# Six ScalarE copies and one in-place transpose instead of six VectorE transposes, for each pair of heads

## The chip, the cores and the metric

The kernel runs on one core of a Trainium2 chip. The metric is the device time of one execution in microseconds (us). A core has five engines with a queue each, worked off in order: TensorE (PE in the profile, with PEld for its weight loads), VectorE (DVE), ScalarE (ACT), GpSimd (POOL) and SyncE (SP, which here issues nearly all DMAs). An instruction that waits holds up everything behind it on its own engine.

## The reference

Eight batches of 576 tokens go through windowed attention with eight heads of 64, and the result through a feed-forward layer. Cut to what matters:

```
masks = [rel >= 0 and rel < 32]  for heads 0-3,  [0 <= rel < 128 and rel % 4 == 0]  for heads 4-7
attn  = softmax(where(mask, q @ k.T / 8, -1e9))        # 576 x 576 for each batch and head
x     = (attn @ v), heads side by side                 # 4608 tokens x 512
g     = elu(x @ w_in)                                  # w_in 512 x 2048
out   = g @ w_out                                      # w_out 2048 x 512
```

Every query sees 32 keys, so a group of 32 queries needs 64 neighbouring keys only (for the dilated heads after a reordering of the tokens).

## The kernel before

**Feed-forward.** The 4608 tokens make nine chunks of 512. Operands are split into a rounded high part and a rest (`wh`, `wl`, `xh`, `xl`, `gh`, `gl`), so that three fast products stand for one exact one. Chunks 0 to 2 do this tile by tile over the 16 blocks of the hidden layer (`product1`, `elu`, `second_product`): PE makes a hidden block in a PSUM bank (`h0`), ACT copies it to SBUF (`L716`, tile `h`), exp and relu (`L721`, `L730`) and a VectorE step (`L731`) make the elu, ACT casts it to `gh` (`L735`), VectorE takes the rest `gl` (`L736`), and two blocks later PE multiplies them with `w_out` into four banks `o_ps`, one for each 128 tokens. At the end of a chunk ACT copies the four banks out (`store`, `L755`, `e<-o_ps`), and the next chunk's products start in the same four banks. Chunks 3 to 6 (`combined_chunk`) use a seven-product scheme (Strassen's) in four groups a chunk: products go to the banks `h0` and `h1`, ACT copies `h0` between products (`e<-h`), and queued second products fill the time between them. Chunks 7 and 8 are done together by `wide_chunks`.

**Attention.** Batch 0 is done at the start, batch 1 inside chunk 0, batches 2 and 3 inside chunks 1 and 2, batches 4 to 7 from the end of chunk 2 to chunk 6. Heads go in pairs, four pairs a batch. For a pair, PE makes scores; VectorE adds the mask into `sm`, 96 partitions (3 groups of 32 queries) x 12 (2 heads x 6 units) x 64 keys; max, subtract, exp (ACT), sum, reciprocal and a multiply make the probabilities (`L415` in `normalise`, or the last 0.9 step of `later_probabilities`). PE then needs them with keys on the partitions: tile `pt`, 128 keys x 12 units x 96 queries, two of them (`pt0`, `pt1`, taken in turn by `transposed`). Group `c` of 32 queries fills column block `c` at partition blocks `c` and `c+1`; all else in `pt` stays at the zeros that were written once at the start. Before the change, VectorE makes each of these six pieces by a transpose from `sm` to `pt` (32 partitions x 12 x 32). In batch 1 this is `L544`, in batches 2 and 3 `L558` (`softmax`, a generator whose steps the main loop draws block by block through `spread`), in batches 4 to 7 it comes from `later_probabilities` (`L573` is the line of a helper, `Ordered`, through which all engine calls of chunks 3 to 8 pass).

**What sets the order.** All matmuls, and everything issued through `Ordered` or `inorder`, stand in program order. The rest (`softmax`, `elu` of chunks 1 and 2, `store`) is placed on its engine by the framework's scheduler, from its own estimate, held only by `issue_after` hints. In chunks 3 to 6 the attention steps wait in a list `side`; at the `w` marks of `TODO` the function `work` takes steps until their listed costs use up the budget in `SPARE`. Steps of pairs 2 and 3 from the transposes on lie in `held` until the outputs of pairs 0 and 1 are issued. `sm` is a single buffer for chunk-1 and chunk-2 pairs.

Of the kernel before, what the change touches and what calls it, by code (L numbers as in the profile page):

```python
# [25 lines left out]
G = 32  # L26
# [60 lines left out]
def body(ctx: ExitStack, tc: tile.TileContext, q, k, v, masks, w_in, w_out, out, out_t):  # L87
    nc = tc.nc
# [101 lines left out]
    def slots(name, *at):  # L190

        step = at[1] - at[0] if len(at) > 1 else 1
        return room_of(name)[:, at[0]:at[-1] + 1:step, :]
# [153 lines left out]
    last_transpose = [None] * B  # L347
# [64 lines left out]
    def normalise(eng, sm, sums, keep):  # L412
        keep(nc.vector.tensor_scalar(out=sums, in0=sums, scalar1=1e-9, scalar2=None, op0=ALU.add))
        keep(nc.vector.reciprocal(out=sums, in_=sums))
        return keep(eng.tensor_tensor(out=sm, in0=sm, in1=sums.unsqueeze(2).broadcast_to([QB, 2 * NU, 2 * G]), op=ALU.mult))  # L415

    def transposed():
        count[0] += 1
        return pt[count[0] % len(pt)]
# [78 lines left out]
    def masks_added(hp, places, sm, eng=nc.vector):  # L498

        dil = hp >= NPAIR // 2  # L500
        for i in range(max(len(p) for p in places)):
            for h in range(2):
                n0, n1, s_ps = places[h][i]
                last = eng.tensor_tensor(out=sm[:, h * NU + n0:h * NU + n1, :].rearrange("p n j -> p (n j)"), in0=s_ps[:QB, :(n1 - n0) * 2 * G],
                                        in1=mask_sb[:, int(dil), n0 * 2 * G:n1 * 2 * G], op=ALU.add)
        return last

    def exponentials(b, hp, places, sm=None):

        if sm is None:  # L510
            sm = ap.tile([QB, 2 * NU, 2 * G], F32, name="sm", bufs=1)
            last = masks_added(hp, places, sm)
            if b == 1:
                masked.append(last.ins)
        nmx = ap.tile([QB, 2 * NU], F32, name="nmx", bufs=4)
        sums = ap.tile([QB, 2 * NU], F32, name="sums", bufs=4)
        with tc.issue_after(rests[0] if (b, hp) == (1, 0) else masked[-1]):
            nc.vector.tensor_reduce(out=nmx, in_=sm, op=ALU.max, axis=mybir.AxisListType.X)
        if b == 1:

            maxima.append(nc.vector.tensor_scalar(out=nmx, in0=nmx, scalar1=-0.125, scalar2=None, op0=ALU.mult).ins)
            if hp > 0:
                for u in range(NU):
                    exponential(u, sm, nmx, sums)
        else:
            nc.vector.tensor_tensor(out=sm, in0=sm, in1=nmx.unsqueeze(2).broadcast_to([QB, 2 * NU, 2 * G]), op=ALU.subtract)
            nc.scalar.activation(out=sm, in_=sm, func=AF.Exp, scale=0.125)
            nc.vector.tensor_reduce(out=sums, in_=sm, op=ALU.add, axis=mybir.AxisListType.X)
        return b, hp, sm, nmx, sums

    def probabilities(b, hp, sm, nmx, sums):
# [12 lines left out]
                    last_transpose[b] = nc.vector.transpose(out=tr[ks, :, cs], in_=sm[cs, :, rs]).ins  # L544
        return b, hp, tr

    spread = []

    def softmax(b, hp, places, tr):

        _, _, sm, _, sums = exponentials(b, hp, places)
        normalise(nc.vector, sm, sums, lambda ins: ins)
        yield
        for c in range(GU):
            for r in range(2):
                ks, cs, rs = slice((c + r) * G, (c + r + 1) * G), slice(c * G, (c + 1) * G), slice(r * G, (r + 1) * G)
                with tc.issue_after(low[-1]):
                    last_transpose[b] = nc.vector.transpose(out=tr[ks, :, cs], in_=sm[cs, :, rs]).ins  # L558
                if (c, r) == (1, 0):
                    yield  # L560
        yield

    def three():
# [11 lines left out]
    vec, act = Ordered(nc.vector), Ordered(nc.scalar)  # L575
    side, held = [], []
# [8 lines left out]
    def later_probabilities(b, hps, groups):  # L585

        other_sm = slots("a5", 2, 3).rearrange("p o t -> p (o t)")[:QB, :2 * NU * 2 * G].rearrange("p (u j) -> p u j", u=2 * NU)
        sms = [ap.tile([QB, 2 * NU, 2 * G], F32, name="sm", bufs=1), other_sm]
        for j in (1, 0):
            masks_added(hps[j], groups[j], sms[j], vec)  # L590
        small = [[ap.tile([QB, 2 * NU], F32, name=n, bufs=4) for n in ("nmx", "sums")] for _ in hps]
        trs = [transposed() for _ in hps]
        wide = lambda x: x.unsqueeze(2).broadcast_to([QB, 2 * NU, 2 * G])

        def steps(j):

            sm, (mx, sums), tr = sms[j], small[j], trs[j]
            yield 0.9, lambda: vec.tensor_reduce(out=mx, in_=sm, op=ALU.max, axis=mybir.AxisListType.X)
            yield 0.9, lambda: vec.tensor_tensor(out=sm, in0=sm, in1=wide(mx), op=ALU.subtract)
            yield 0.0, lambda: act.activation(out=sm, in_=sm, func=AF.Exp, scale=0.125)  # L600
            yield 0.9, lambda: vec.tensor_reduce(out=sums, in_=sm, op=ALU.add, axis=mybir.AxisListType.X)
            yield 0.1, lambda: vec.tensor_scalar(out=sums, in0=sums, scalar1=1e-9, scalar2=None, op0=ALU.add)
            yield 0.1, lambda: vec.reciprocal(out=sums, in_=sums)
            yield 0.9, lambda: vec.tensor_tensor(out=sm, in0=sm, in1=wide(sums), op=ALU.mult)
            for c in range(GU):
                for r in range(2):
                    ks, cs, rs = slice((c + r) * G, (c + r + 1) * G), slice(c * G, (c + 1) * G), slice(r * G, (r + 1) * G)
                    yield 0.57, lambda ks=ks, cs=cs, rs=rs: vec.transpose(out=tr[ks, :, cs], in_=sm[cs, :, rs])

        one, other = list(steps(0)), list(steps(1))  # L610
        side.extend([*one[:2], other[0], one[2], other[1], one[3], other[2], *one[4:7], *other[3:7]])
        (held if hps[0] else side).extend(one[7:] + other[7:])
        return [(b, hp, tr) for hp, tr in zip(hps, trs)]

    def scores_piece(b, hps, between=None):
# [23 lines left out]
        if b <= CS:  # L639
            trs = [transposed() for _ in hps]  # L640
            made = [(b, hp, tr) for hp, tr in zip(hps, trs)]
            one, other = [softmax(b, hp, groups[j], trs[j]) for j, hp in enumerate(hps)]
            next(one)
            spread.extend(((one,), (one, other), (other,), (other,)))
        else:
            made = later_probabilities(b, hps, groups)
# [23 lines left out]
    hidden, below, low, high = [], [], [], []  # L670
# [824 lines left out]
```

## Time and profile before

| | |
|---|---|
| median of three runs | 854.6 us (854.01 to 854.99) |
| the profiled execution | 853.85 us |
| its span, first to last instruction | 852.0 us |
| PE busy, matmuls | 839.9 us (99%) |
| PE weight loads | 704.0 us (83%) |
| VectorE busy | 657.6 us (77%), 993 instructions |
| ScalarE busy | 486.5 us (57%), 835 instructions |
| chain of waits, share of PE | 97% |

The times in the tables of the trace are those of the one profiled execution. A row gives a start, a length, the engine, the line, what is written from what, the size and a count; in brackets stands how long the engine had been idle before it and what ended that. A matmul row's length includes its passage through the array, so that consecutive matmuls overlap: what counts for PE is the distance from start to start.

### The profile page before, as it was taken

What the parts mean: (1) busy time and instruction counts of PE and PEld (TensorE: products, weight loads), DVE (VectorE), ACT (ScalarE), POOL (GpSimd) and SP (SyncE); (2) the same over time, 40 slices, a digit from 0 to 9 for tenths busy, and PEclk for the clock granted to TensorE, in tenths of its full rate; (3) what the DMA queues carried; (4) which work ended last, traced back from release to release, by engine and by line L of the source; (5) the groups of instructions that cost most, each with busy time, mean ns of one, the idle gap of its engine ahead of it and who ended that gap; (6) DMA issues with size and microseconds to landing.
All of it is one profiled execution on the core that took longest, in us unless ns stands there. A gap on an engine that the chain in (4) does not pass through costs nothing.

```text
span 852.0 us, 17515 instructions
## 1 busy us (share of the span) xinstructions
PE 839.9 (99%) x7080; PEld 704.0 (83%) x7080; DVE 657.6 (77%) x993; ACT 486.5 (57%) x835; POOL 8.7 (1%) x29
## 2 busy tenths in 40 slices
PE   6999999999999999999999999999999999999998
PEld 4566888888888889898999899899989988888886
DVE  5999998778588978965877587757877765786992
ACT  5889776645655465434644464544544556786460
POOL 3000000000000000000000000000000000000000
PEclk9999999999999999999999999999999999999999
DMA  8997457533677878757586667767675667997675
GB/s 301 378 378 304 138 170 237 163 112 107 204 253 237 266 206 258 242 181 244 179 262 195 193 219 221 251 186 218 193 237 189 212 209 240 334 353 247 188 222 170
DMA packets 99728, 193.73 MB, mean 227 GB/s; under 512 B 8800, under 2 KB 52160, under 8 KB 99648
## 3 DMA queue, kind: packets, MB, share of 16 engines
q1 hardware_dynamic: 99504, 192.30, 69.5%
q8 instruction: 56, 0.92, 0.4%
q10 hardware_dynamic: 144, 0.31, 0.1%
q14 instruction: 24, 0.20, 0.1%
HBM read 145.39 MB, written 47.19 MB: 226 GB/s over the span
## 4 chain that ended last, share of the span: by engine, by line
PE 97%; DMA 1%; ACT 1%; DVE 1%; issue 0%; SPq 0%; DVEq 0%; POOL 0%; ACTq 0%
PE o_ps L124 44%; PE h L124 41%; PE a_ps L124 11%; DMA r<-w_in 1%; DMA qt<-q 0%; ACT pt L490 0%; DVE nmx L450 0%; PE a L124 0%; DVE pt L488 0%; PE b L124 0%; PE d L124 0%; DVE sums L469 0%; ACT r L467 0%; DVE gh L573 0%; ACT x L404 0%
## 5 line engine op out<-in xcount | busy, mean ns | idle before, releaser
L124 PE MATMUL h<-xh,r 128*128 128x256 f32 (+1 forms) x728 | 171.7, 315 | 0.0
L124 PEld LDWEIGHTS h<-xh,r 128*128 128x128 f32 x728 | 123.6, 190 | 10.5 <-issue 0.2
L124 PE MATMUL o_ps<-a,r 128*128 128x512 f32 x528 | 127.0, 391 | 0.0
L124 PEld LDWEIGHTS o_ps<-a,r 128*128 128x128 f32 x528 | 97.3, 188 | 19.2
L124 PE MATMUL h<-xl,r 128*128 128x256 f32 (+1 forms) x364 | 109.0, 315 | 0.0
L124 PE MATMUL h<-a,r 128*128 128x256 f32 (+1 forms) x492 | 77.7, 308 | 0.0
L124 PE MATMUL o_ps<-a,gh 128*128 128x512 f32 x216 | 75.0, 444 | 0.0
L124 PEld LDWEIGHTS h<-a,r 128*128 128x128 f32 x492 | 69.6, 190 | 6.6
L124 PEld LDWEIGHTS h<-xl,r 128*128 128x128 f32 x364 | 69.3, 190 | 5.7 <-issue 0.2
L573 DVE SCALAR_TENSOR_TENSOR a-1_3460<-a-1_3460,a 128x1024 f32<-128x1024 f32 x32 | 39.1, 1222 | 37.3 <-ACT a L573 37.2
L573 ACT COPY e<-h 128x512 f32<-128x512 f32 x48 | 28.2, 588 | 56.3 <-PE h L124 55.5
L124 PE MATMUL o_ps<-r,r 128*128 128x512 f32 x220 | 57.5, 390 | 0.0
L124 PEld LDWEIGHTS o_ps<-a,gh 128*128 128x128 f32 x216 | 40.2, 188 | 17.3 <-issue 10.5
L573 DVE TENSOR_TENSOR a-1_3460<-h,e 128x512 f32<-128x512 f32 x48 | 33.0, 688 | 26.1 <-PE h L124 25.4
L124 PEld LDWEIGHTS o_ps<-r,r 128*128 128x128 f32 x220 | 40.6, 188 | 8.0
L573 ACT COPY a-1_3460<-h 128x512 f32<-128x512 f32 x16 | 9.4, 586 | 56.2 <-PE h L124 56.2
L124 PE MATMUL h<-r,r 128*128 128x256 f32 (+1 forms) x252 | 40.6, 311 | 0.0
L573 ACT ACTIVATE a<-a 128x1024 f32<-128x1024 f32 (+1 forms) x40 | 40.0, 1017 | 0.9
L716 ACT COPY h<-h 128x512 f32<-128x512 f32 x30 | 17.5, 584 | 39.8 <-PE h L124 39.6
L124 PE MATMUL o_ps<-r,gh 128*128 128x512 f32 x128 | 40.1, 395 | 0.0
L736 DVE TENSOR_TENSOR gl<-e,gh 128x512 fp32r<-128x512 f32 x37 | 25.4, 687 | 17.6 <-ACT gh L735 17.2
L124 PE MATMUL o_ps<-a,a 128*128 128x512 f32 x156 | 38.9, 391 | 0.0
(266 smaller groups left out, 1711.1 us busy)
## 6 DMA issues: line engine op xcount, KB each, us to landing
r<-combined SPq DMA_DIRECT2D x140, 512.0 KB, 4.4
vt<-v SPq DMA_DIRECT2D x30, 384.0 KB, 4.5
kt<-k SPq DMA_DIRECT2D x29, 304.0 KB, 4.3
qt<-q SPq DMA_DIRECT2D x30, 288.0 KB, 3.7
r<-w_in SPq DMA_DIRECT2D x16, 512.0 KB, 7.0
r<-w_out SPq DMA_DIRECT2D x16, 512.0 KB, 8.0
r<-sums_out SPq DMA_DIRECT2D x16, 512.0 KB, 4.7
r<-plain_out SPq DMA_DIRECT2D x12, 512.0 KB, 4.7
```

What stands on the lines that cost most here:

```text
L124: return inorder(nc.tensor.matmul(*args, **kw))
L573: return lambda *args, **kw: inorder(getattr(self.eng, name)(*args, **kw))
L716: copied.append(a.copy(out=h, in_=h_ps).ins)
L736: low.append(v.tensor_tensor(out=gl, in0=e, in1=gh.bitcast(F32), op=ALU.subtract).ins)
```

## The change

For batches 2 to 7 (24 pairs of heads) each of the six VectorE transposes becomes a ScalarE copy of the same 32 x 12 x 32 piece to the same place in `pt`, not yet transposed (`placed`). One VectorE transpose over the whole of `pt` (128 partitions x 1152), with the same tile as input and output, then turns every 32 x 32 block in place (`turned`). Blocks of zeros stay zeros. Batch 1 keeps its six transposes.

```diff
+    def placed(tr, sm, c, r, eng):
+
+        return eng.copy(out=tr[(c + r) * G:(c + r + 1) * G, :, c * G:(c + 1) * G], in_=sm[c * G:(c + 1) * G, :, r * G:(r + 1) * G])
+
+    def turned(tr, eng):
+
+        flat = tr.rearrange("p u q -> p (u q)")
+        return eng.transpose(out=flat, in_=flat)
+
     def softmax(b, hp, places, tr):
...
         yield
         for c in range(GU):
             for r in range(2):
-                ks, cs, rs = slice((c + r) * G, (c + r + 1) * G), slice(c * G, (c + 1) * G), slice(r * G, (r + 1) * G)
-                with tc.issue_after(low[-1]):
-                    last_transpose[b] = nc.vector.transpose(out=tr[ks, :, cs], in_=sm[cs, :, rs]).ins
-                if (c, r) == (1, 0):
-                    yield
+                with tc.issue_after(high[-1]):
+                    placed(tr, sm, c, r, nc.scalar)
+        yield
+        with tc.issue_after(low[-1]):
+            last_transpose[b] = turned(tr, nc.vector).ins
         yield
...
             for c in range(GU):
                 for r in range(2):
-                    ks, cs, rs = slice((c + r) * G, (c + r + 1) * G), slice(c * G, (c + 1) * G), slice(r * G, (r + 1) * G)
-                    yield 0.57, lambda ks=ks, cs=cs, rs=rs: vec.transpose(out=tr[ks, :, cs], in_=sm[cs, :, rs])
+                    yield 0.3, lambda c=c, r=r: placed(tr, sm, c, r, act)
+            yield 1.4, lambda: turned(tr, vec)
...
-        (held if hps[0] else side).extend(one[7:] + other[7:])
+        (held if hps[0] else side).extend(one[7:-1] + other[7:-1] + one[-1:] + other[-1:])
```

The new functions shift the lines below them by nine: `L716` to `L755` of before are `L725` to `L764` now, and `L573` is `L582`. The order of PE's instructions is the same in both programs. On ScalarE and VectorE it is not. At the start of chunk 1, ScalarE had this order before (`a_` and `r_` are weight tiles; the four `e<-o_ps` copies empty the output banks of chunk 0):

```order
L721 ACTIVATE e<-h 128x512
L755 COPY e<-o_ps 128x512 x3
L730 ACTIVATE e<-e 128x512
L716 COPY h<-h_1690 128x512
L755 COPY e<-o_ps 128x512
L721 ACTIVATE e<-h 128x512
L735 CAST gh<-e 128x512
```

and has this one now:

```order
L730 ACTIVATE e<-h 128x512
L764 COPY e<-o_ps 128x512 x3
L739 ACTIVATE e<-e 128x512
L549 COPY pt_80<-sm 32x12x32 x6
L725 COPY h<-h_1693 128x512
L764 COPY e<-o_ps 128x512
L744 CAST gh<-e 128x512
```

The six copies of the first pair of batch 2 stand ahead of the copy of the hidden block and of the fourth output bank's copy. At the first group of chunk 3, ScalarE had before (`a_2290` is the exp tile of the elu, and later the second pair's probabilities; `h_3843` is bank `h0`):

```order
L573 ACTIVATE a_2290<-a_2290 128x1024
L755 COPY e<-o_ps 128x512
L573 COPY e<-h_3843 128x512
L573 CAST r_1178<-a-1_3460 128x1024
L755 COPY e<-o_ps 128x512
L573 ACTIVATE a_2290<-a-1_3460 128x1024
L755 COPY e<-o_ps 128x512 x2
L573 ACTIVATE a_2290<-a_2290 128x1024
L573 COPY e<-h_3843 128x512
```

and has now:

```order
L582 COPY pt_80<-sm 32x12x32 x4
L764 COPY e<-o_ps 128x512
L582 CAST r_1178<-a-1_3468 128x1024
L582 COPY pt_80<-sm 32x12x32
L582 COPY e<-h_3853 128x512
L582 ACTIVATE a_2294<-a-1_3468 128x1024
L764 COPY e<-o_ps 128x512 x2
L582 ACTIVATE a_2294<-a_2294 128x1024
L582 COPY pt_80<-sm 32x12x32
L582 COPY pt_79<-a_2294 32x12x32 x3
L764 COPY e<-o_ps 128x512
L582 COPY e<-h_3853 128x512
```

Five copies into `pt` and a cast stand ahead of the bank's copy `e<-h`, and nine in all ahead of the fourth `e<-o_ps`. The other pairs of batches 2 and 3 show six copies in a row, each time behind an exp or relu (`L730`, `L739`) of a hidden block and ahead of ScalarE's next copy or cast.

## The prediction

> **What bounds the kernel now.** I read the page first, its busy times and the chain of waits:
>
> ```profile
> PE 839.9 (99%) x7080; PEld 704.0 (83%) x7080; DVE 657.6 (77%) x993; ACT 486.5 (57%) x835; POOL 8.7 (1%) x29
> PE 97%; DMA 1%; ACT 1%; DVE 1%; issue 0%; SPq 0%; DVEq 0%; POOL 0%; ACTq 0%
> ```
>
> PE is the path: 97% of the chain that ended last is PE working. Where it idles is told by the view by windows (length, then PE, PEld, DVE, ACT, POOL busy, the granted clock and the DMAs):
>
> ```profile
> 0.00:30.00 30.00, 21.64 (x494) 16.45 (x494) 20.88 (x40) 18.33 (x59) 7.58 (x17) 0.94 0.91 311
> 126.00:325.00 199.00, 198.96 (x1724) 163.49 (x1723) 156.97 (x280) 114.60 (x210) 0.48 (x5) 1.00 0.64 201
> 325.00:690.00 365.00, 365.00 (x3472) 328.02 (x3471) 271.19 (x412) 183.33 (x259) 0.67 (x7) 1.00 0.69 216
> ```
>
> Of 12.1 us that PE is not busy, 8.4 lie in the first 30 us, ahead of the change. From 126 to 690 us, where all 24 changed pairs are worked, PE lacks 0.04 us of 564. VectorE is busy 79% and 74% there, and what it saves cannot shorten a queue that never waits for it. So the question is only whether ScalarE, busy 58% and 50%, can take the copies without making PE wait.
>
> **What the change costs each engine.** The groups by line and shape give the prices (count, busy us, mean ns):
>
> ```profile
> L573 DVE STREAM_TRANSPOSE pt<-a 32x384 f32<-32x384 f32 x48 | 27.3, 568 | 0.8
> L558 DVE STREAM_TRANSPOSE pt<-sm 32x384 f32<-32x384 f32 x48 | 27.3, 568 | 0.7
> L573 DVE STREAM_TRANSPOSE pt<-sm 32x384 f32<-32x384 f32 x48 | 27.2, 568 | 0.8
> L573 DVE SCALAR_TENSOR_TENSOR a-1_3460<-a-1_3460,a 128x1024 f32<-128x1024 f32 x32 | 39.1, 1222 | 37.3 <-ACT a L573 37.2
> L686 ACT CAST xh<-x 128x384 fp32r<-128x384 f32 x4 | 2.0, 508 | 0.0
> L490 ACT COPY pt<-c 32x192 f32<-32x192 f32 x8 | 2.5, 311 | 0.2
> L755 ACT COPY e<-o_ps 128x512 f32<-128x512 f32 x12 | 6.5, 588 | 4.5 <-DMA out<-e 3.8 <-PE o_ps L124 0.7
> ```
>
> VectorE loses 144 transposes of 568 ns, 81.8 us. One of 1152 elements a partition replaces six of 384. At no more than 1222 / 1024 = 1.19 ns an element, from the nearest long VectorE row, 768 more elements make 568 + 914 = 1.48 us, 36 us for 24 pairs; VectorE gains 46 us. The bound below is a single 568 (if the length did not count), the bound above six times 568, 3.4 us, if the width in partitions counted.
>
> ScalarE gains 144 copies of 384 elements a partition from SBUF to SBUF. The nearest row is the cast of 128x384, 508 ns. Below it lies the 192-element copy with 311 ns, above it the 512-element one with 588. What a copy occupies also depends on how it overlaps with its neighbour:
>
> ```profile
> 15.67 2.65 ACT L490 COPY pt<-c 64x192 f32<-64x192 f32 x8
> 140.08 1.54 ACT L755 COPY e<-o_ps 128x512 f32<-128x512 f32 x3
> ```
>
> Three full-width copies of 588 take 1.54, a step of 0.48: each starts 0.1 before its forerunner ends. Eight copies into `pt`, which move from one partition block to another, take 2.65, a step of 0.33 for a length of 0.31: no overlap. The new copies move on by a block, on one side or the other, each time, so I take 0.51 + 0.02 = 0.53 as their step, 3.2 us for six. 144 x 0.508 are 73 us of busy time more for ScalarE, which would stand at 66%.
>
> The Trainium skill (ScalarE: Activation LUTs, What ACT_TABLE_LOAD costs) gives an ACTIVATE 186 ns + 0.833 ns an element and lets neighbours overlap by about 93 ns. By it a copy of 384 would take 506 ns, as the 508 row says, but step by 0.41; the `pt<-c` row contradicts the overlap for this kind of copy.
>
> **Where 3.2 us in one piece reach PE.** The scheduler puts the copies behind ScalarE's work for one hidden block and ahead of the next copies that free a PSUM bank. All later rows of the queue wait. I go through the tight places; elsewhere the copy behind them isn't wanted for longer.
>
> *A, start of chunk 1: the fourth output bank.*
>
> ```profile
> 140.82 0.95 DVE L415 TENSOR_TENSOR sm<-sm,sums 96x768 f32<-96x768 f32 x1
> 141.50 0.64 ACT L730 ACTIVATE e<-e 128x512 f32<-128x512 f32 x1
> 142.71 0.59 ACT L716 COPY h<-h 128x512 f32<-128x512 f32 x1 [0.56 <-PE h L124]
> 143.19 0.59 ACT L755 COPY e<-o_ps 128x512 f32<-128x512 f32 x1
> 144.32 0.41 PEld L124 LDWEIGHTS o_ps<-r,gh 128*128 128x128 f32 x2
> 144.55 0.62 PE L124 MATMUL o_ps<-r,gh 128*128 128x512 f32 x2
> ```
>
> Today the bank is empty at 143.78, and PE loads weights for it at 144.32 (0.23 ahead of its matmul): cover 0.54, and 0.56 of idle before `h`. Now six copies start at 142.04 and end at 142.04 + 5 x 0.53 + 0.51 = 145.20; `h` runs 145.22 to 145.81, the bank's copy 145.71 to 146.30. PE is late by **2.0**.
>
> *B, 247 us: bank `h0`, which chunks 1 and 2 have once.*
>
> ```profile
> 241.76 0.64 ACT L730 ACTIVATE e<-e 128x512 f32<-128x512 f32 x1
> 243.31 0.95 DVE L415 TENSOR_TENSOR sm<-sm,sums 96x768 f32<-96x768 f32 x1
> 247.13 0.39 PE L124 MATMUL h<-xh,a 128*128 128x512 f32 x1
> ```
>
> ScalarE is free at 242.40, but the copies wait for the probabilities, ready at 244.26. Six run to 247.45, then `h` to 248.06; PE wants the bank at 246.90. That is 1.2 late at most; VectorE, with less to do, may have the probabilities sooner. I take **1.0**, from 0.4 up.
>
> *C, 298 us: the cast `gh`.*
>
> ```profile
> 290.62 0.85 ACT L527 ACTIVATE sm<-sm 96x768 f32<-96x768 f32 x1 [2.20 <-DVE sm L526]
> 294.58 0.63 ACT L730 ACTIVATE e<-e 128x512 f32<-128x512 f32 x1
> 294.68 0.95 DVE L415 TENSOR_TENSOR sm<-sm,sums 96x768 f32<-96x768 f32 x1
> 295.12 0.60 ACT L735 CAST gh<-e 128x512 fp32r<-128x512 f32 x1
> 297.99 0.61 PE L124 MATMUL o_ps<-a,gh 128*128 128x512 f32 x2
> 298.65 0.50 PE L124 MATMUL o_ps<-a,gl 128*128 128x512 f32 x1
> ```
>
> With the probabilities at 295.63 the copies end at 298.82 and the cast, now behind them, at 299.46, for a weight load at 297.76: 1.7 late. But here VectorE is the late one (the exp waited 2.20 us for it), and it has lost 2 us of work a pair, so the copies start earlier. Between 0 and 1.7 I take **0.8**.
>
> *D and E, first group of chunk 3.*
>
> ```profile
> 333.54 1.06 ACT L573 ACTIVATE a<-a 128x1024 f32<-128x1024 f32 x1
> 335.35 0.59 ACT L755 COPY e<-o_ps 128x512 f32<-128x512 f32 x1 [0.74 <-PE o_ps L124]
> 336.78 0.59 ACT L573 COPY e<-h 128x512 f32<-128x512 f32 x1 [0.85 <-PE h L124]
> 337.26 1.05 ACT L573 CAST r<-a-1_3460 128x1024 fp32r<-128x1024 f32 x1
> 339.65 1.08 ACT L755 COPY e<-o_ps 128x512 f32<-128x512 f32 x2
> 338.65 1.59 PE L124 MATMUL h<-a,r 128*128 128x256 f32 x12
> 340.08 2.91 PE L124 MATMUL o_ps<-a,r 128*128 128x512 f32 x12
> ```
>
> The relu ends at 334.60. In the new order follow four copies (to 336.60), an output bank (337.21), the cast (337.11 to 338.16), the fifth copy (338.69) and `e<-h` (339.30), which PE wants at 338.42: **0.9** (D). Then exp (to 340.39), two output banks (341.37), relu (342.36), four copies (344.48), and the fourth output bank, at 345.09. PE comes to its fourth block of three matmuls at 340.08 + 9 x 0.227 - 0.23 = 341.9, with D at 342.8: **2.3** (E).
>
> In the later chunks the order puts four copies ahead of the third `e<-h` of a group, and eight behind it. The chain, merged, gives the room:
>
> ```profile
> 396.62 2.75 PE o_ps L124 x12
> 399.37 2.87 PE h L124 x24
> ```
>
> 24 matmuls are two products, 1.44 each. The bank is wanted again two products and 12 second products later, 2.87 + 2.75 = 5.6 us, for 4 x 0.53 + 0.6 = 2.7 us of ScalarE. That cover holds; if it went, each of the seven such places would cost what the copies exceed it by.
>
> VectorE's other new wait: the next pair's mask add (`L504`) needs `sm`, which the copies now hold until they end, and the in-place transpose waits for the sixth copy. Behind both stand only `L731`, `L736` and the softmax itself, and the outputs come six blocks later; I cost it at nothing, at up to 1 us if the transpose took 3.4.
>
> SP issues in order too: the stores `out<-e` of A and E wait for the late bank copies, and the loads behind them by up to 3 us.
>
> ```profile
> r<-combined SPq DMA_DIRECT2D x140, 512.0 KB, 4.4
> ```
>
> Those loads are issued four products ahead and land in 4.4 us; four products with their second products last over 8 us by the two chain rows, so this too costs nothing unless the delay passes 3.6 us.
>
> Sum: 2.0 + 1.0 + 0.8 + 0.9 + 2.3 = 7.0 us. PE has no slack behind these places, so nothing is caught up. The profiled execution would go from 853.85 to 860.9; the median of before lies 0.75 above its profiled execution, so I predict **861.6** (chance 0.66, from 859 to 865). With 0.61 a copy (the 588 row) A to E make about 9.3, with 0.33 (the 311 row) about 2.0: 863.9 and 856.6.
>
> **The rivals.** *The copies overlap* (0.16): step 0.41, and the copy behind starts 0.12 earlier too. A shrinks to 1.2, B and C to 0.3 together, D and E to 2.0: 3.5 us, **858.1**. For it: full-width copies overlap. Against it: the `pt<-c` row, though its source is PSUM. The Trainium skill's overlap, given above, points the same way.
>
> *The cover holds* (0.10), not slower: ScalarE takes the copies into its idle time, and VectorE's 46 us end the little lateness that the trace puts on it, as with `gl` at 298.65 (0.50 instead of 0.39). Price: below 0.5 us in all, **854.1**. It decides only if six copies fit the 1.1 us of cover at A, 0.18 a copy, which is below every row shown. The Trainium skill (Perfetto Trace Analysis, Identifying the Most-Contended Engine) says that matmul busy time is no measure of headroom and to go by weight loads, 83% here, which would leave PE far more to win. Against it the merged row above: 12 matmuls of 512 columns in 2.75 us, one every 0.23, the same distance as inside every full batch.
>
> *The transpose or ScalarE's load bites more* (0.08): at 3.4 us a transpose, or with copies late in the later groups too, 3 to 5 us more, around **866**.
>
> **How the numbers follow.** About 0.2% (1.7 us) is what a measurement of this kernel can tell from no change. The forecast, the overlap and the third rival are slower by more: 0.90. The cover's 0.10 I split into 0.07 the same and 0.03 faster. The range 857 to 865 leaves out the cover and most of the third rival.
>
> **What would show it.** Right: ScalarE copies `pt<-sm` near 508 ns, stepping by 0.53; PE gaps near 144, 247, 298, 338 and 342 us, ended by ACT (or long matmul rows there), nothing new after 345; VectorE's busy time down by about 46 us. Wrong: a copy step of 0.41 or less, PE whole at A and E, or PE waiting for `pt` itself.

## The result: 9.0 us slower

| | before | with the change |
|---|---|---|
| median of four runs | 854.62 us (854.01 to 854.99) | 863.65 us (862.82 to 864.90) |
| ratio, 95% interval | | 1.0108 (1.009 to 1.0125) |
| profiled execution | 853.85 us | 863.18 us |
| its span | 852.0 us | 861.3 us |
| predicted | | 861.6 us, 857 to 865 |

The kernel became slower, as forecast, and by 2 us more than forecast. The busy times and the chain of waits of the new page:

```profile
PE 840.9 (98%) x7080; PEld 702.4 (82%) x7080; DVE 607.1 (70%) x873; ACT 559.0 (65%) x979; POOL 8.7 (1%) x29
...
PE 80%; DVE 7%; ACT 6%; DMA 4%; issue 2%; DVEq 0%; SPq 0%; ACTq 0%
```

VectorE lost 50.5 us of work and ScalarE gained 72.5. PE has the same 840 us to do, but it is no longer the whole chain. The groups by line and shape of the new kernel show what the new operations cost:

```profile
L549 ACT COPY pt<-sm 32x384 f32<-32x384 f32 x48 | 24.4, 509 | 4.1 <-DVE sm L415 3.6
...
L582 DVE STREAM_TRANSPOSE pt<-pt 128x1152 f32<-128x1152 f32 x16 | 21.9, 1370 | 3.3 <-ACT pt L582 3.3
```

A copy takes 0.51 us, a turn 1.37. Now the five places. These are PE's rows of the new kernel's timeline (start, length, and in brackets how long PE had nothing in its array, and what ended that):

```profile
146.50 0.73 PE L124 MATMUL o_ps<-r,gh 128*128 128x512 f32 x2 [1.88 <-ACT e L764]
...
250.77 0.50 PE L124 MATMUL h<-xh,a 128*128 128x512 f32 x1 [1.34 <-ACT h L725]
...
302.58 0.73 PE L124 MATMUL o_ps<-a,gh 128*128 128x512 f32 x2 [0.61 <-ACT gh L744]
...
344.11 1.69 PE L124 MATMUL h<-a,r 128*128 128x256 f32 x12 [0.65 <-ACT e L582]
...
349.84 1.47 PE L124 MATMUL o_ps<-a,r 128*128 128x512 f32 x3 [1.98 <-ACT e L764]
```

They are A, B, C, D and E of the prediction, each ended by ScalarE with the copy or cast that was named. The bracket counts from the end of the last matmul's passage, which overlaps the next start by 0.16 (a matmul row is 0.39 long where one starts every 0.23), so PE lost 0.16 more than it says: 2.04, 1.50, 0.77, 0.81 and 2.14, together 7.3 us. To this each restart adds about 0.1 (the two matmuls behind a gap take 0.73, where they took 0.62 at 144.55 before; the single one 0.50 instead of 0.39). The prediction's own rows tell the same from another side: the matmul of A started at 144.55 before and starts at 146.50 now, that of B at 247.13 and 250.77, of C at 297.99 and 302.58, of D at 338.65 and 344.11.

So far the span would be 7.8 us longer. It is 9.3, and the rest stands right behind E. The view by windows (window, then its length and PE, PEld, DVE, ACT, POOL busy, the granted clock and the DMAs) of the new kernel:

```profile
346.65:350.05 3.40, 1.42 (x7) 0.88 (x6) 2.52 (x2) 3.30 (x7) 0.00 (x0) 1.00 0.92 234
350.05:353.45 3.40, 3.40 (x77) 2.38 (x77) 0.50 (x1) 2.80 (x5) 0.10 (x1) 0.50 0.36 136
353.50:356.90 3.40, 3.40 (x86) 2.71 (x85) 1.40 (x3) 0.00 (x0) 0.00 (x0) 1.00 0.02 5
```

For 3.4 us after the wait at E the granted clock is 0.50. The same matmuls start 7.70 us later than before at the beginning of this stretch and 9.21 later at its end: **1.5 us**, which no term of the prediction had. From there on to the end of the kernel the distance stays between 9.2 and 9.4. All this is the one profiled execution; the other three show a mean granted clock of 0.993 or 0.994 where this one has 0.998, which is about two more stretches of 3.4 us at half clock, and no trace tells where these lay.

What stands ahead of the late bank copies on ScalarE, at A and at D and E, from the new kernel's timeline:

```profile
142.24 3.11 ACT L549 COPY pt<-sm 32x384 f32<-32x384 f32 x6
145.37 0.59 ACT L725 COPY h<-h 128x512 f32<-128x512 f32 x1
145.86 0.59 ACT L764 COPY e<-o_ps 128x512 f32<-128x512 f32 x1
...
342.94 0.51 ACT L582 COPY pt<-sm 32x384 f32<-32x384 f32 x1
343.47 0.59 ACT L582 COPY e<-h 128x512 f32<-128x512 f32 x1
...
347.09 0.51 ACT L582 COPY pt<-sm 32x384 f32<-32x384 f32 x1
347.62 1.55 ACT L582 COPY pt<-a 32x384 f32<-32x384 f32 x3
349.20 0.59 ACT L764 COPY e<-o_ps 128x512 f32<-128x512 f32 x1
```

Six copies take 3.11 us: (3.11 - 0.51) / 5 is a step of 0.52, with no overlap. At A the bank is empty at 146.45, and PE starts at 146.50; at E it is 349.79 and 349.84.

### The profile page after: what moved, and what is told of

Its sections match the earlier page's. It is cut to its first block, busy times and chain, and to the rows that moved or that the text cites. A ratio compares the mean times of both kernels' runs of the same rounds, so it can differ in the third digit from the quotient of the medians.

```text
span 861.3 us, 17540 instructions
## 1 busy us (share of the span) xinstructions
PE 840.9 (98%) x7080; PEld 702.4 (82%) x7080; DVE 607.1 (70%) x873; ACT 559.0 (65%) x979; POOL 8.7 (1%) x29
## 4 chain that ended last, share of the span: by engine, by line
PE 80%; DVE 7%; ACT 6%; DMA 4%; issue 2%; DVEq 0%; SPq 0%; ACTq 0%
PE o_ps L124 36%; PE h L124 33%; PE a_ps L124 10%; DMA qt<-q 1%; DMA r<-w_out 1%; DVE pt L544 1%; ACT pt L549 1%; DMA r<-w_in 1%; ACT e L764 1%; DVE a L177 1%; DMA out<-e 0%; ACT sm L496 0%; DVE gl L745 0%; DVE r L216 0%; ACT h L725 0%
## 5 line engine op out<-in xcount | busy, mean ns | idle before, releaser
L582 DVE SCALAR_TENSOR_TENSOR a-1_3468<-a-1_3468,a 128x1024 f32<-128x1024 f32 x32 | 39.1, 1223 | 50.5 <-ACT a L582 50.5
L582 DVE TENSOR_TENSOR a-1_3468<-h,e 128x512 f32<-128x512 f32 x48 | 33.1, 689 | 42.6 <-PE h L124 42.0
L582 ACT COPY e<-h 128x512 f32<-128x512 f32 x48 | 28.2, 588 | 46.9 <-PE h L124 41.8
L582 ACT ACTIVATE a<-a 128x1024 f32<-128x1024 f32 (+1 forms) x40 | 40.0, 1017 | 0.9
L124 PEld LDWEIGHTS h<-r,r 128*128 128x128 f32 x252 | 35.7, 190 | 4.0 <-issue 0.3
L124 PE MATMUL a_ps<-a,r 128*128 128x512 f32 x156 | 37.3, 389 | 0.0
```

Of the source, the lines that this page charges most:

```text
L124: return inorder(nc.tensor.matmul(*args, **kw))
L582: return lambda *args, **kw: inorder(getattr(self.eng, name)(*args, **kw))
```

## The experiments

The theory is the prediction's: the time is lost at five places, because of what stands behind the copies in ScalarE's queue. Its main rival is that more work on ScalarE, or more traffic, costs something wherever it stands. In what was expected, the half clock is put at 1.1 us, which was my first reading; the rows above give 1.5.

### One half of the pairs alone

In the first kernel `softmax` (batches 2 and 3) is that of before again, in the second the steps of `later_probabilities` (batches 4 to 7) are:

```diff
# late batches only, in softmax; the second kernel undoes the change to later_probabilities in the same way
-                with tc.issue_after(high[-1]):
-                    placed(tr, sm, c, r, nc.scalar)
-        yield
-        with tc.issue_after(low[-1]):
-            last_transpose[b] = turned(tr, nc.vector).ins
+                ks, cs, rs = slice((c + r) * G, (c + r + 1) * G), slice(c * G, (c + 1) * G), slice(r * G, (r + 1) * G)
+                with tc.issue_after(low[-1]):
+                    last_transpose[b] = nc.vector.transpose(out=tr[ks, :, cs], in_=sm[cs, :, rs]).ins
+                if (c, r) == (1, 0):
+                    yield
```

> Only batches 4 to 7 keep the copies and the turn in place; batches 2 and 3 have their six VectorE transposes again. *Five places* (mine: the time is lost where copies stand in ScalarE's queue ahead of a copy or cast that PE wants): A 2.0, B 1.5 and C 0.8 vanish, D 0.8 and E 2.1 stay, and so does the stretch of half clock behind E, which costs about 1.1: 854.6 + 4.1 = 858.7 us, PE waiting only at D and E in 126 to 690 us. *Rival, spread load* (the cost lies in ScalarE's load and in SBUF traffic, and goes with the number of copies wherever they stand): 16 of 24 pairs keep theirs, two thirds of 9.0, so 860.6 us, with PE's gaps spread thinly.

> Only batches 2 and 3 keep the copies; batches 4 to 7 have their VectorE transposes again. *Five places*: A 2.0, B 1.5, C 0.8 stay, D and E vanish, and with them the half clock behind E: 854.6 + 4.3 = 858.9 us. *Spread load*: 8 of 24 pairs, a third of 9.0: 857.6 us. The two terms of this run and of the one with the late batches alone should add up to the whole, 9.0, by either; a shortfall of about 1 would say that the half clock needs both.

Measured against 854.15 us for before: 858.51 us with the late batches alone, ratio 1.0045 (1.0027 to 1.0063), and 858.63 with the early ones, 1.005 (1.0031 to 1.0069). That is 4.4 and 4.5 us, together 8.8 of the 9.0. The five places ask for 4.1 and 4.3, the spread load for 6.0 and 3.0: with twice as many pairs the late batches do not cost more than the early ones. By the intervals the late batches cost 2.3 to 5.4 us and the early ones 2.6 to 5.9, so that the spread load's 6.0 is ruled out and its 3.0, taken alone, is not. PE and windows of the kernel with the late batches alone:

```profile
345.22 1.61 PE L124 MATMUL o_ps<-a,r 128*128 128x512 f32 x3 [1.96 <-ACT e L764]
```

```profile
17.65:21.00 3.35, 3.35 (x45) 3.32 (x43) 3.25 (x7) 1.98 (x6) 1.16 (x2) 0.50 1.03 357
...
341.90:345.25 3.35, 1.39 (x7) 0.80 (x6) 2.52 (x2) 3.25 (x7) 0.00 (x0) 1.00 0.99 281
345.30:348.70 3.40, 3.40 (x76) 2.48 (x77) 0.37 (x1) 2.92 (x5) 0.10 (x1) 0.50 0.28 104
```

With the late batches alone PE also waits 0.47 us at 630 us; the profile names no releaser, and this wait is not explained. E is the same to 0.02 us, and so is the half clock behind it; the only other stretch of half clock ahead of the kernel's last 4 us is one of the start-up, the first row. In the kernel with the early batches alone there is none after the start-up; of the places that it shares with the full change, B differs most. ScalarE's rows of the early batches alone, then of the full change:

```profile
240.96 0.59 ACT L764 COPY e<-o_ps 128x512 f32<-128x512 f32 x1 [3.76 <-DMA out<-e]
...
246.37 3.12 ACT L549 COPY pt<-sm 32x384 f32<-32x384 f32 x6 [1.90 <-DVE sm L415]
```

```profile
241.58 0.59 ACT L764 COPY e<-o_ps 128x512 f32<-128x512 f32 x1 [4.34 <-DMA out<-e]
...
246.99 3.12 ACT L549 COPY pt<-sm 32x384 f32<-32x384 f32 x6 [1.90 <-DVE sm L415]
```

The fourth bank of chunk 1 is copied out into a buffer that an earlier store must leave first. With that store 0.6 us later, exp, sum, probabilities and copies are all 0.6 later, and PE's loss at B is 1.5 instead of 0.9. Before, the same wait was 3.78. In the four other kernels whose batches 2 and 3 are those of before, it is 3.64 to 4.30, so it differs by as much between executions in which nothing was changed there.

### The copies moved out of the way

All copies stay on ScalarE, in other places of its queue:

```diff
# softmax: all six one step (a yield) later, behind the last copy of an output bank (stores) and the cast
-                with tc.issue_after(high[-1]):
+                with tc.issue_after(stores[-1]), tc.issue_after(high[-1]):
                     placed(tr, sm, c, r, nc.scalar)
# work(spare, copies_left) stops when a step's copies are used up; the keys are chunk, group and step
-                        work(SPARE[g][s])
+                        work(SPARE[g][s], {(CS, 0, 5): 3, (CS, 0, 6): 0, (CS, 1, 0): 0}.get((c, g, s), 99))
```

> All 24 pairs keep copies and turn; only their places in ScalarE's queue move. In batches 2 and 3 all six copies stand behind the cast of the hidden block and the output bank's copy that they stood ahead of; in the first group of chunk 3 three copies instead of four stand ahead of the first bank, none ahead of `e<-h` and of the fourth bank, and nine go in one piece behind the next cast. *Five places*: PE waits nowhere in 126 to 690 us for more than 0.3 us, the half clock behind E is gone, 854.6 us, from 854.2 to 855.5. *Spread load*: as many copies, so 863 us as with the change. *A third theory, VectorE's turn is late for PE* (the transpose waits for the last copy, now later still): PE would wait for `pt` in some of the places, 1 us or more each.

Measured: 863.0 us, ratio 1.0099 (1.0081 to 1.0118). That is the time of the spread load, and my forecast of 854.6 was wrong. The profile does not bear the spread load out, though. A to E are gone, and two other long waits have come in their place, beside a short one of 0.44 us at 205 us, where six copies now stand ahead of ScalarE's copy of `h`. PE's rows of this kernel, from two windows of its timeline:

```profile
306.20 0.88 PE L124 MATMUL a_ps<-pt,vt 128*64 128x96 f32 x16 [2.23 <-DVE pt L554]
...
356.39 0.36 PE L124 MATMUL h<-xh,r 128*128 128x256 f32 x1 [3.06 <-issue]
```

VectorE's rows of the same kernel tell where they come from:

```profile
304.76 1.38 DVE L554 STREAM_TRANSPOSE pt<-pt 128x1152 f32<-128x1152 f32 x1 [2.33 <-ACT pt L549]
...
354.27 1.38 DVE L582 STREAM_TRANSPOSE pt<-pt 128x1152 f32<-128x1152 f32 x1 [1.76 <-ACT pt L582]
355.57 0.71 DVE L582 TENSOR_TENSOR a<-h,masks_sb 96x256 f32<-96x256 f32 x2
```

At 306 us the turn, held up until the sixth copy, is late for the outputs: the third theory. At 356 us it is the wait that the prediction costed at nothing: the mask add of the next pair cannot start while the copies hold its buffer (they end at 354.24) and the turn stands ahead of it, and PE needs the bank of scores that the mask add reads. "Issue" in PE's row says that no releaser was found; the mask add that reads this bank begins at 355.57 with two pieces, and ends 0.1 before PE goes on. Behind this gap, too, the clock is halved:

```profile
353.40:356.75 3.35, 0.36 (x3) 0.40 (x4) 2.48 (x6) 1.41 (x3) 0.00 (x0) 1.00 0.88 280
356.80:360.15 3.35, 3.35 (x15) 3.06 (x14) 3.09 (x5) 0.00 (x0) 0.00 (x0) 0.50 0.67 212
```

The three waits with their restarts and the half clock make about 8 of the 9.7 us by which this kernel's span is longer; the rest is spread in steps of 0.5 us and less, and its cause is open.

So order decides, but simply later is not better: the copies stand between two deadlines. What comes behind them on ScalarE is one, and the turn and the next mask add, which wait for them, are the other.

### Only where there is room

Two kernels give pairs back their VectorE transposes, first the five pairs that stand at A to E, then all of batches 2 and 3 and the first two pairs of batch 4:

```diff
+BACK = (2, 0), (3, 0), (3, 3), (4, 0), (4, 1)     # five pairs back
+BACK = (4, 0), (4, 1)                             # fourteen pairs, with softmax as before
...
+                    if (b, hps[j]) in BACK:
+                        yield 0.57, lambda ks=ks, cs=cs, rs=rs: vec.transpose(out=tr[ks, :, cs], in_=sm[cs, :, rs])
+                    else:
+                        yield 0.3, lambda c=c, r=r: placed(tr, sm, c, r, act)
```

> The five pairs whose copies stand at A (first pair of batch 2), B and C (first and fourth of batch 3), D and E (first two of batch 4) get their six VectorE transposes back; the other 19 keep copies and turn, 114 of 144 copies. *Five places*: all of the loss is gone, the time is that of before, 854.2 us, from 853.7 to 855.0, and PE waits nowhere from 126 to 690 us. *Spread load*: 19 of 24 of the loss stays, 854.2 + 7.1 = 861.3 us. Nothing in either theory makes it faster than before, since PE lacks nothing there that VectorE's saved time could give.

Measured: 855.76 us, 1.0014 (1.0005 to 1.0023). Of 9.0 us 1.35 are left, where the spread load asks for 7.1. They are not at A to E. PE's row of this kernel, and VectorE's ahead of it:

```profile
299.78 0.50 PE L125 MATMUL o_ps<-a,gl 128*128 128x512 f32 x1 [0.76 <-DVE gl L763]
```

```profile
295.50 2.90 DVE L563 STREAM_TRANSPOSE pt<-sm 32x384 f32<-32x384 f32 x5
...
299.04 0.69 DVE L763 TENSOR_TENSOR gl<-e,gh 128x512 fp32r<-128x512 f32 x1
```

My way of giving them back put six transposes in one piece where before had two of three, and `gl` behind them is 0.9 late. A further gap of 0.6 us at 627 us has no releaser in the profile; like the one at 630 us with the late batches alone, it is not explained.

> Batches 2 and 3 have before's code again, transposes, hints and steps, and so have the first two pairs of batch 4; the other 14 pairs, worked from the third group of chunk 3 on, keep copies and turn (84 of 144 copies). It is the kernel with five pairs back without that kernel's own loss: there six transposes in one piece made PE wait 0.92 us for `gl` at 299 us, which before's two pieces of three did not. *Five places*: the time of before within 0.1%, 854.4 us, and no gap over 0.3 us that ends with ScalarE or VectorE from 126 to 690 us. *Spread load*: 14/24 of 9.0, 859.6 us.

Measured: 854.71 us against 854.82, 0.9996 (0.9987 to 1.0005): no difference. Its window from 325 to 700 us:

```profile
325.00:700.00 375.00, 375.00 (x3517) 336.27 (x3517) 246.93 (x349) 229.99 (x348) 0.67 (x7) 1.00 0.69 215
```

The same window of before:

```profile
325.00:700.00 375.00, 375.00 (x3516) 336.31 (x3515) 276.49 (x419) 187.64 (x264) 0.67 (x7) 1.00 0.69 215
```

PE is whole, VectorE has 30 us less to do and ScalarE 42 us more in these 375 us. 84 copies cost nothing, and 30 us off VectorE gain nothing.

### VectorE as the copier

```diff
-                    placed(tr, sm, c, r, nc.scalar)     # eng.copy
+                    placed(tr, sm, c, r, nc.vector)     # eng.tensor_copy, held by low[-1] instead of high[-1]
-                    yield 0.3, lambda c=c, r=r: placed(tr, sm, c, r, act)
+                    yield 0.3, lambda c=c, r=r: placed(tr, sm, c, r, vec)
```

> All 24 pairs are placed and turned in place, but VectorE makes the six copies, not ScalarE: ScalarE's queue is that of before. *Five places* (the loss is ScalarE's order alone, not the turn in place and not the traffic): 854.2 us, with at most 0.5 more where VectorE is the late one; VectorE's busy time is 607 + 144 times a copy, which no row shows yet: with 0.3 us 650 us, with 0.5 680 us, both below the 99% of PE. *Rival, the turn in place or the longer way through SBUF costs*: 858 us or more, with PE waiting for `pt`.

Measured: 855.08 us, 1.0006 (0.9996 to 1.0015). With ScalarE's queue as before, all 24 pairs placed and turned cost nothing that can be told; the one new wait is 0.6 us for `pt` in batch 3. A group by shape of this kernel:

```profile
L549 DVE COPY pt<-sm 32x384 f32<-32x384 f32 x48 | 16.8, 350 | 0.7
```

VectorE copies a piece in 0.35 us where ScalarE takes 0.51, and six copies with a turn, 3.47 us, are no cheaper for it than six transposes, 3.41.

### How much room there is

```diff
-                        yield 0.3, lambda c=c, r=r: placed(tr, sm, c, r, act)
+                        yield 0.3, lambda c=c, r=r: [placed(tr, sm, c, r, act) for _ in range(2)]             # five pairs back, doubled
+                        yield 0.3, lambda c=c, r=r: [placed(tr, sm, c, r, act) for _ in range(1 + (c == 2))]  # fourteen pairs, eight copies
```

> As the kernel with five pairs back, but in batches 5 to 7 and in the last two pairs of batch 4 each copy is made twice in a row, 84 copies more, 44 us of ScalarE. It tests the cover that the prediction put at 5.6 us in the later groups. *Cover holds*: ahead of the third `e<-h` of a group stand eight copies now, 8 x 0.52 + 0.6 = 4.8 us against 5.6, so PE waits for none of them: within 0.5 us of the other kernel. *Cover was smaller than I thought* (only one product and its second products count, 1.44 + 1.4): 2 us late in each of seven groups, 14 us more. *Spread load*: 84 x 9.0 / 144 = 5.3 us more.

Measured: 900.27 us, 1.053 (1.0514 to 1.0545), 44.5 us over five pairs back, and 84 copies of 0.53 are 44.5 too. All three expectations were far too low. What PE waits for in this kernel (us in total, times, longest):

```profile
PE o_ps L125 <- DVE r L596: 11.2, 2, 6.2
PE h L125 <- DVE a-1_3465 L596: 7.8, 4, 2.7
PE h L125 <- ACT e L596: 6.9, 3, 2.3
PE o_ps L125 <- DVE a L596: 6.4, 1, 6.4
```

Only 6.9 us of these 32 are waits for ScalarE itself. The longest are for the rest of a hidden block (the tiles `r` and `a` here) on VectorE. Its rows at the first of them:

```profile
442.38 1.38 DVE L596 STREAM_TRANSPOSE pt<-pt 128x1152 f32<-128x1152 f32 x1 [8.46 <-ACT pt L596]
443.69 1.18 DVE L596 TENSOR_TENSOR a<-a-1_3465,a 128x1024 fp32r<-128x1024 f32 x1
```

The turn waits 8.46 us for the last copy, and the rest that PE wants stands behind it: the same kind of wait as with the copies moved. Each of three chunks has three gaps, a tenth stands at 704 us, and in or behind five of them the clock is halved, which costs about 9 us more. So the agreement with the full length of the copies is one of totals; no row shows PE waiting a copy's length for each copy. The prediction's cover of 5.6 us was read at the third `e<-h` of a group. The tight places lie at the end of a chunk.

> As the kernel with fourteen pairs, but the last two of each pair's six copies are made twice, so eight a pair, 28 copies or 14.7 us of ScalarE more. With all six made twice each copy more cost PE its whole 0.52 us. *A margin that was nearly used up* (mine, after that run): at the end of a chunk `e<-h` is copied by 431.53 us in the kernel with five pairs back and PE's next product into that bank starts at 432.65, so with the weight load about 0.9 us are left; two more copies take 1.04 there and in three chunks PE is late by 0.1 to 0.3 us each: 0 to 1 us over the kernel with fourteen pairs. *No margin, each copy costs its length*: 14.7 us more. *The cover of 5.6 us as I predicted it*: nothing at all.

Measured: 855.68 us, 1.0016 (1.0007 to 1.0025), 1.0 over the fourteen pairs. ScalarE's row and PE's, from this kernel's timeline:

```profile
523.65 0.59 ACT L583 COPY e<-h 128x512 f32<-128x512 f32 x1
```

```profile
524.29 1.45 PE L125 MATMUL h<-a,r 128*128 128x256 f32 x10
```

`e<-h` ends at 524.24 and PE starts 0.05 later; the matmul starts 0.13 us behind its usual distance. The same stands in the chunk before, at 431.61 us, and in the next, at 616.96. So 0.9 us of room was right, and two copies more overfill it. With the slower restart (0.11 us, as at A to E) the three places make 0.7 of the 1.0 us; for the rest the profiled execution shows no place.

### What a copy costs, and the half clock

Three copies in a row keep their partition blocks, by reading block 0 and writing block 0, then three by block 1:

```diff
-        return eng.copy(out=tr[(c + r) * G:(c + r + 1) * G, :, c * G:(c + 1) * G], in_=sm[c * G:(c + 1) * G, :, r * G:(r + 1) * G])
+        return eng.copy(out=tr[r * G:(r + 1) * G, :, c * G:(c + 1) * G], in_=sm[r * G:(r + 1) * G, :, r * G:(r + 1) * G])
# and the loops in the order r, c
```

> The six copies keep their size, number and place in the queue, but three in a row read partition block 0 and write block 0, and the next three read and write block 1, each into another column block (the probabilities are put in the wrong places, so the attention's output is not the reference's). *Blocks moving keeps copies from overlapping* (my reading of step 0.53): within each three the step falls to 0.41 to 0.43, six copies take 2.7 instead of 3.1 us, A, B and C each shrink by 0.4, D and E together by about 0.6, 863.6 - 1.8 = 861.8 us. *Rival: 32 partitions or SBUF to SBUF is what forbids the overlap*: step 0.52 as before and 863.6 us.

Measured: 860.31 us, 1.0066 (1.0049 to 1.0084), 6.2 over before instead of 9.0. ScalarE at A, PE at E and the windows there:

```profile
142.51 2.67 ACT L549 COPY pt<-sm 32x384 f32<-32x384 f32 x6
```

```profile
349.00 0.73 PE L124 MATMUL o_ps<-a,r 128*128 128x512 f32 x2 [1.62 <-ACT e L764]
```

```profile
346.00:349.35 3.35, 1.73 (x9) 1.10 (x8) 2.51 (x2) 3.30 (x8) 0.00 (x0) 1.00 0.82 209
349.40:352.80 3.40, 3.40 (x84) 2.54 (x82) 1.04 (x1) 2.31 (x5) 0.10 (x1) 1.00 0.44 171
```

Six copies take 2.67 instead of 3.11. With 0.52 for the one step that changes the block (the trace has 0.52 between the third and the fourth start), the other four are (2.67 - 0.51 - 0.52) / 4 = 0.41. So it is the changing block that forbids the overlap, and not the 32 partitions or the way from SBUF to SBUF; nor is it that a copy writes another block than it reads, since neither the third nor the fourth copy does. The waits at A to E are 1.15, 1.06, 0.18, 0.43 and 1.62 in brackets, 2.0 less in all than with the change, where 1.8 was expected, though not 0.44 at each place. A new one of 0.26 stands at 244 us, behind an output bank's copy that waited 5.08 us for the store named at B. The half clock, 1.5 us, did not follow E here. Together that is the size of the 2.9 us that this kernel is faster than the change. Two copies less at E test that further:

```diff
# late batches only, and the first two copies of the second pair of batch 4 left out
-                    yield 0.3, lambda c=c, r=r: placed(tr, sm, c, r, act)
+                    yield 0.3, lambda c=c, r=r: None if (b, hps[j], c) == (4, 1, 0) else placed(tr, sm, c, r, act)
```

> As the kernel with the late batches alone, but two of the four copies that stand ahead of the fourth output bank at E are left out (the first two of the second pair of batch 4, so that pair's probabilities are incomplete). *Each copy is 0.52 us of PE*: E falls from 2.1 to 1.1, D stays 0.8. *Half clock by idle time in one stretch of 3.41 us*: gaps of 2.13 and 2.14 us at E were followed by half clock for 3.41 us, one of 1.78 us was not; at 1.1 us it stays away, in every run, so 858.5 - 1.05 - 0.8 (about the mean of the stretch over the runs) = 856.7 us. *Rival, the half clock comes from something else at that place*: it is seen again behind E, 857.5 us.

Measured: 856.93 us, 1.0027 (1.0015 to 1.004), against 856.7 expected. PE's row at E, and the windows up to there and behind:

```profile
343.84 0.97 PE L124 MATMUL o_ps<-a,r 128*128 128x512 f32 x3 [0.92 <-ACT e L764]
```

```profile
340.00:344.00 4.00, 3.08 (x18) 2.37 (x17) 1.86 (x2) 3.93 (x8) 0.00 (x0) 1.00 0.73 178
344.00:348.00 4.00, 4.00 (x92) 2.84 (x98) 1.70 (x2) 2.85 (x5) 0.10 (x1) 1.00 0.56 218
```

E is 1.04 shorter for two copies (0.92 instead of 1.96 with the late batches alone), and the clock stays whole behind it. This holds for the profiled execution, the fastest of six (855.64 to 858.82). Its mean granted clock was 1.000, that of the others 0.997 or 0.998, and no trace tells where they lost it. The interval, 855.7 to 857.8 us, holds the rival's 857.5 too, so it is the trace that speaks against the rival, and not the time.

## Why the prediction was right, and where it was short

- **PE as the bound, and nothing to be won on VectorE**: right. Fourteen pairs take 30 us off VectorE and the time does not move.
- **The copy, 0.51 long and stepping by 0.53**: 0.509 and 0.52. The rival with overlap fell for the reason that was given, the changing block; where the block stays, the step is the 0.41 that the rival had. The Trainium skill (ScalarE: Activation LUTs, What ACT_TABLE_LOAD costs) has 93 ns of overlap between neighbours; 0.51 - 0.41 = 0.10 agrees with it for copies that stay in their block, and the 0.52 of the changed kernel does not.
- **The turn, 1.48**: 1.37, inside its bounds. VectorE saved 50 us, not 46, and none of it mattered.
- **A 2.0, D 0.9, E 2.3**: 2.0, 0.8 and 2.1. The order of the queue and the lengths of its rows were enough for these. Two small misses cancel in A: the copies began at 142.24 and not at 142.04, and PE started 0.05 us after the bank was empty, where the prediction had counted a weight load of 0.23 behind it.
- **C 0.8, between 0 and 1.7**: 0.8; that the figure fits so well is luck, since it was taken from the middle. The direction was right: measured against PE's matmuls, which are 3.8 us later here than before, the probabilities came 1.8 us sooner (VectorE's multiply starts at 296.72, where it was 294.68). The copies still started at 298.77 only, when ScalarE was through with the relu that stands at 294.58 in the prediction's rows, and the prediction took no bound from that relu.
- **B 1.0, from 0.4 to 1.2**: 1.5 in the profiled execution and 0.9 in the kernel with the early batches alone. The step that failed is "VectorE, with less to do, may have the probabilities sooner": they came no sooner in either kernel, because their time hung on ScalarE's wait for a store, which differs between executions, and not on VectorE's load.
- **Sum 7.0**: the five places made 7.3 and the restarts behind them 0.5. What the sum lacked is the half clock behind E, 1.5 us in the profiled execution. "Nothing new after 345" failed by this one stretch. Without it the profiled execution would have come to 861.7; it came to 863.18, and the median lies 0.5 above it.
- **The cover in the later chunks**: the outcome was right, the reason was not. The 5.6 us at the third `e<-h` are not the tightest place; at the end of a chunk 0.9 us are left, and doubled copies cost 44.5 us, 17.6 of it in waits for what stands behind the turn, which waits for the last copy.
- **The next mask add and the turn, costed at nothing**: right for the order in the change. With the copies later they became waits of 3.1 and 2.2 us.
- **The late stores and the loads behind them, costed at nothing**: right. From 126 us to the end of the kernel PE's only waits are the five.
- **The cover holds**, and **more than forecast at the turn**: neither came true. The 2 us above the forecast look like the third rival's size, but PE waited for `pt` nowhere in the batches that were changed.

## What to carry to other kernels

A low busy share of an engine (57% here) does not make room for work in one piece: look up what stands behind the new instructions in that engine's queue, and by when the path needs it, and then what waits for the new instructions themselves, since moving them back only trades the one for the other. Where TensorE already works all the time, relief for another engine is worth nothing. After a wait of TensorE of some 2 us, look at the granted clock behind it before the time is put down to something else.

## What the runs showed of the hardware

**Half clock after a gap of 2 us.** In stretches of 3.41 us, laid on a fixed grid, the granted clock is either 1.00 or 0.50. With the late batches alone such stretches begin at 17.61 and 345.30 us, 327.69 apart, which is 96 times 3.413. A stretch in which PE worked 1.42 of 3.40 us (E with the change), 1.39 of 3.35 (late batches alone) or 0.36 of 3.35 (copies moved) was followed by one at 0.50; one with 1.73 of 3.35 (steady blocks) was not. With the early batches alone A's gap fell into one stretch (144.71 to 148.12 us), PE worked 1.68 of 3.35 us there, and nothing followed either. With the change, A's gap of 2.04 us fell across the border of two stretches, and nothing followed; the new kernel's windows there:

```profile
141.90:145.25 3.35, 2.72 (x13) 1.91 (x11) 0.77 (x2) 3.29 (x7) 0.00 (x0) 1.00 1.04 361
145.30:148.70 3.40, 2.20 (x10) 1.80 (x11) 3.28 (x7) 3.32 (x7) 0.00 (x0) 1.00 0.85 279
```

So whether a gap of this size costs 1.5 us more depends on where it falls on the grid, which differs between executions: the stretch of half clock in the start-up begins at 17.61 us with the late batches alone and at 18.25 before. The Trainium skill (TensorE: Matmul & The Clock Gate, What's actually happening) knows the window of 3413 ns that runs freely, and puts half clock behind an idle one; the length and the grid agree with these runs, but here a window in which PE worked four tenths of the time was enough.

**Overlap of ScalarE's copies** goes with the partition block: 0.41 us from start to start for copies that read and write the block of their forerunner, 0.52 for copies of the same size where the block of the input or of the output changes.
